# A fused delta-rule attention and two mixture-of-experts layers: the second layer's weight splits issued after the routing search's steps, and its last slot finished tile by tile

## The chip, the cores and the metric

One core of a Trainium2 chip. The metric is the device time of one execution in microseconds; three runs of the kernel before gave 959.33, 962.1 and 964.19, median 962.1.

## The reference, cut to what matters

Three stages follow one another: a delta-rule attention over 3072 tokens, a first expert layer, and a second expert layer, which is the one that the change touches. In it every token goes to one of 8 experts, each of which takes exactly 384 tokens; token and expert pairs are taken in falling order of their logits.

```python
cap = N // E                      # 3072 // 8 = 384
logits = x @ w_gate
for idx in np.argsort(-logits.flatten()):
    tok, e = int(idx) // E, int(idx) % E
    if assigned[tok] >= 0 or counts[e] >= cap:
        continue
    assigned[tok] = e
    counts[e] += 1
for e in range(E):
    mask = assigned == e
    h = np.maximum(x[mask] @ w1[e], 0.0)      # 384 -> 1024
    out[mask] = h @ w2[e]                     # 1024 -> 384
```

## The kernel before, in words

The second layer (`layer2`) runs eight *slots*, one per expert, in the order in which experts fill up. A *router* finds them: a *phase* of it searches the logit threshold at which the next expert is full (`search`), closes that expert (`close`) and lists its tokens (`listing`). A search has four *steps*. In each, DVE makes an index (`sf`, line 1382) and two comparison tables (`cmp`, 1333), PE counts with 24 small matmuls (`pr` <- `cmp`, 1341), DVE thresholds the counts (`reach`, 1345), PE spreads the result with one matmul (1351), and DVE reduces it (`reached`, 1355); then comes the next step's `sf`. After the fourth step `close` starts with `sel` (1474) and ends in `new` (1481), which a PE matmul waits for (1489). `listing` makes `clv` on DVE, from it POOL makes the expert's number `ei` (1541), SyncE (SP) reads that and issues four loads of 768 KB (`raw`, 1031 and 1034); later DVE makes `mrk` and `he`, PE lists (1570) and DVE writes the token indices `lidx` (1578).

A slot (`ffn`) is 48 *points*. A point is three matmuls of 384 columns, either part of the first product (`g1`, `ph` <- `xT`, line 1077; three points make one of eight blocks f) or of the second (`g2`, `po` <- `HL,hh`, line 1097; per block f and token tile t). A product is three matmuls because weights and activations are held as a high and a low part. After a block's third `g1` point ACT writes the high part of the activation `hh` (1080) and DVE the low part (1085, `h_low`). There are two `ph` buffers, so block f+2 cannot start before DVE has done block f's low part. `g2` of block f comes two blocks later (`LAG`); the last two blocks come at the end, tile by tile.

At every point `tasks(pt)` may put one piece of other work into the engines' queues: the router's next piece (`next(r)`; the numbers that the router yields, table `WT`, say how many points to let pass: the second is the wait from `cmp` to the count, the third from the count to `reach`), the loads (`load_ahead`), the gather of the next slot's tokens (`xg`) and its three transposes (`trans`, `xT`), and the *splits*. Each engine works its queue in order.

A split (`split_w`, lines 1047 and 1048) turns half a loaded piece of 128 x 1536 into its high part (ACT copies, `HL` <- `raw`) and its low part (subtraction `raw` - high, on DVE or on POOL). Eight splits j = 0 to 7 make the weights of one slot; they are done during the slot before, into the other of two `HL` buffers. In the kernel before, a slot's splits start 10 points after its four loads were put in the queue (2 points into the slot if that was at point 0 or earlier), are spread evenly to point 46, and the low part goes to POOL for j other than 1 and 5, to DVE for these two. In slot 0's own weights the two engines alternate. At a slot's end `finish2` copies the three output tiles `x` <- `po` (1594, 1596) and POOL issues three scatters (`out_dram`, 1599).

Of the kernel before, what the change touches and what calls it, by code (L numbers as in the profile page):

```python
# [35 lines left out]
class Attention:  # L36
# [369 lines left out]
    def go(self, w_gate, side=iter(())):  # L406
# [160 lines left out]
J = 64  # L567
STEPS = 4
LAG = 2
WT = [(5, 4, 1, 2, 3, 3, 1), (5, 4, 1, 2, 3, 3, 1), (5, 4, 1, 2, 3, 3, 1), (5, 4, 1, 2, 3, 2, 2),  # L570
      (5, 4, 1, 2, 3, 2, 2), (5, 4, 1, 2, 3, 3, 2), (5, 4, 1, 2, 6, 3, 2), (5, 4, 1, 2, 7, 4, 2)]
PRO = 16
SPQ, TRQ = (3, 10), (11, 12, 12)
XW = 19
# [1 line left out]
HEAT = (2, 5, 6, 7, 9)  # L576
HEAT1 = (3, 1, 1, 1, 0)
BEFORE = 10


def run(g):
# [92 lines left out]
class Moe:  # L674
# [421 lines left out]
        for n, (a, b) in enumerate(((0, 0), (0, 1), (1, 0))):  # L1096
            nc.tensor.matmul(self.po[s][t], h[:, a, r], W[:, 2 + i, b, c], start=(f == 0 and n == 0), stop=(f == 7 and n == 2))  # L1097

    def ffn(self, s, tasks):

        pt = 0
        for f in range(8):
            for k in range(3):
                self.g1(s, f, k)
                tasks(pt)
                pt += 1
            self.h_low()
            for t in range(3):
                if f >= LAG:
                    self.g2(s, f - LAG, t)  # L1110
                    tasks(pt)
                    pt += 1
        for t in range(3):
            for f in range(8 - LAG, 8):
                self.g2(s, f, t)
                tasks(pt)
                pt += 1
# [50 lines left out]
    def layer1(self):  # L1168
# [65 lines left out]
        self.logits_add(7)  # L1234
        self.warm(BEFORE)
        with self.tc.For_i(1, n, 1) as j:
# [121 lines left out]
    def search(self):  # L1358


        nc = self.nc
        y = self.small([128, 24], "sy", bufs=2)
        f = self.f = self.small([128, 24], "sf", I16)
        cmp = [None, None]

        def front():
            nc.vector.scalar_tensor_tensor(f, self.key, self.sc, self.low, op0=OP.mult, op1=OP.add)
            self.warm(self.heat[2])
            yield
            cmp[0] = self.compare(f, 0)  # L1370
            yield
            cmp[1] = self.compare(f, 1)
            yield
            nc.vector.scalar_tensor_tensor(y, self.key, self.sc, self.low, op0=OP.mult, op1=OP.add)
            yield

        yield from self.keys(front())
        yield self.W[0]
        for i in range(STEPS):
            pb = self.pb = yield from self.count(cmp, i + 1 == STEPS)  # L1380
            if i + 1 < STEPS:
                nc.vector.tensor_scalar(f, y, pb, float(J), op0=OP.subtract, op1=OP.mult)  # L1382
                cmp = [self.compare(f, h) for h in range(2)]
                if i + 2 < STEPS:
                    y2 = self.small([128, 24], "sy", bufs=2)
                    nc.vector.tensor_scalar(y2, y, pb, float(J), op0=OP.subtract, op1=OP.mult)
                    y = y2
                yield self.W[1]

    def find(self, f, digits):  # L1390
# [214 lines left out]
    def layer2(self):  # L1605
        nc = self.nc
        self.oscat, self.wanted, self.split_at, self.W, self.out_of, self.heat = [], [], 0, WT[0], -1.0e30, HEAT
        self.raw, self.xg, self.xT, self.idx, self.oids = {}, {}, {}, {}, {}

        def split(s, j):  # L1610
            self.split_w(s, j, j % 2 if s == 0 else j % 4 != 1)
            if j % 2:
                self.split_at += 1

        self.L2s = self.c1.tile([128, 24, 8], F32, name="L2s")
        r = self.router()
        next(r)
        nc.gpsimd.tensor_copy(self.L2s, self.L2)
        while 0 not in self.idx:
            next(r)  # L1620
            self.load_ahead()
        self.gather(0, self.x2buf, self.idx[0])
        sp, tr = iter(range(8)), iter(range(3))
        for q in range(PRO):
            next(r)
            self.load_ahead()
            for _ in range(SPQ.count(q)):
                split(0, next(sp))
            for _ in range(TRQ.count(q)):
                t = next(tr)  # L1630
                self.trans(0, t, f"po{t}")
        first = len(SPQ)
        self.heat = (0,) * 5
        for s in range(8):
            at, k, wt, j = None, 0, None, 0

            def tasks(pt):
                nonlocal at, k, wt, j, first
                if s == 0 and first < 8 and pt % 2 == 0:
                    split(0, first)  # L1640
                    first += 1
                next(r, None)
                self.load_ahead()
                if s == 0 and pt == 30:
                    self.oids[0] = self.oid(0)
                if s == 7:
                    return
                if wt is None and len(self.raw.get(s + 1, ())) == 4:
                    wt = 2 if pt == 0 else pt + 10
                elif wt is not None and j < 8 and pt >= wt and not (s == 0 and first < 8):  # L1650
                    split(s + 1, j)
                    j += 1
                    wt = pt + max(2, (46 - pt) // (9 - j))
                if at is None and s + 1 in self.idx:
                    self.gather(s + 1, self.x2buf, self.idx[s + 1])
                    at = max(pt + 10, 24)
                elif at is not None and k < 3 and pt >= at + 5 * k:
                    self.trans(s + 1, k)
                    k += 1

            self.ffn(s, tasks)
            if s < 7:
                while s + 1 not in self.idx:
                    next(r)
                if at is None:
                    self.gather(s + 1, self.x2buf, self.idx[s + 1])
                while j < 8:
                    self.load_ahead()
                    split(s + 1, j)
                    j += 1  # L1670
                while k < 3:
                    self.trans(s + 1, k, "pr" if k == 1 else "pt")
                    k += 1
                self.oids[s + 1] = self.oid(s + 1)
            self.finish2(s)
        self.general()
# [16 lines left out]
    def router(self):  # L1693

        def phase(p):
            if p < 7:
                yield from self.search()
            else:
                yield from self.keys()
                yield  # L1700
            yield from self.close(p)
            yield self.W[6]

        def steps(g):
            for n in g:
                for _ in range(n or 1):
                    yield

        side = iter(())
        for p in range(8):  # L1710
            self.W = WT[p]
            for _ in steps(phase(p)):
                next(side, None)
                yield
            for _ in side:
                yield
            side = steps(self.listing(p))
            if p in (0, 7):
                yield from side
                side = iter(())  # L1720
# [87 lines left out]
```

## Time and profile before

| what | value |
|---|---|
| median of three runs | 962.1 us |
| the profiled execution | 958.21 us, its span 956.3 us |
| second layer's slots | from about 668 us; slot 1 starts at 707.4, slot 5 at 870.6, slot 7 at 923.0, last product at 948 us |
| PE busy, whole span | 833.6 us (87%) |
| POOL low parts in the second layer | 46 splits, 1854 ns each |
| DVE low parts in the second layer | 18 splits, 1312 ns each |

PE, DVE, ACT and POOL are TensorE, VectorE, ScalarE and GpSimd; SPq is SyncE's queue. In a timeline row the first number is the start, the second the length, and the bracket the idle time of the engine before it with the work that ended it. PEclk is the TensorE clock that was granted, as a share of the full 2.4 GHz.

### The profile page before, as it was taken

Reading aid. Unit: us, or ns where it says so; the run is one execution under the profiler, and the core shown is the slowest. Engines: PE = TensorE matmul, PEld = TensorE weight load, DVE = VectorE, ACT = ScalarE, POOL = GpSimd, SP = SyncE. Lnnn points to the kernel's source line nnn. Section 1 sums busy time; section 2 is a strip of 40 time slices with the busy share of each in tenths; the row PEclk is TensorE's granted clock in tenths of the full one; section 3 lists DMA queues with packets and bytes.
Section 4 is the critical chain, followed back from the end, with each engine's and each line's share of the span. In section 5 each row is a group of like instructions: output and inputs, shape, how many; then the busy total and the mean of one; then the engine's idle time right before and its main releaser. Section 6 shows DMA issues by size and latency. Waiting matters only on the chain. (4 is left out here: it accounts for less than half of the span.)

```text
span 956.3 us, 23017 instructions
## 1 busy us (share of the span) xinstructions
PE 833.6 (87%) x9031; PEld 747.0 (78%) x9031; DVE 657.9 (69%) x1716; ACT 454.6 (48%) x990; POOL 381.7 (40%) x532
## 2 busy tenths in 40 slices
PE   5459879888897996999999999987989879989996
PEld 4448769777786885799999999864768768879996
DVE  5997989899797958555745556238767886785331
ACT  4556576675766576344445454221243232333431
POOL 7256345453432022522122221023474556457551
PEclk9878798897888798999999999999999999999998
DMA  9651143351500004563185532203245225326300
GB/s 156 117 99 35 39 90 68 69 106 39 102 19 19 20 28 160 202 207 115 33 296 162 151 115 77 90 29 111 69 145 175 92 92 183 132 66 234 117 25 28
DMA packets 141318, 98.27 MB, mean 103 GB/s; under 512 B 102757, under 2 KB 123268, under 8 KB 141204
## 3 DMA queue, kind: packets, MB, share of 16 engines
q1 hardware_dynamic: 134484, 76.67, 29.7%
q0 software_dynamic: 6720, 20.07, 6.6%
q8 instruction: 74, 1.21, 0.5%
q14 instruction: 40, 0.33, 0.1%
HBM read 82.36 MB, written 14.55 MB: 101 GB/s over the span
## 5 line engine op out<-in xcount | busy, mean ns | idle before, releaser
L1097 PE MATMUL po<-HL,hh 128*128 128x384 f32 x1152 | 235.9, 345 | 0.0
L1077 PE MATMUL ph<-xT,HL 128*128 128x384 f32 x1152 | 231.9, 344 | 3.0 <-ACT xT L1066 1.2
L1077 PEld LDWEIGHTS ph<-xT,HL 128*128 128x128 f32 x1152 | 200.3, 189 | 15.1 <-issue 6.7
L1097 PEld LDWEIGHTS po<-HL,hh 128*128 128x128 f32 x1152 | 199.2, 190 | 3.2 <-issue 1.3
L1080 ACT ACTIVATE hh<-ph 128x384 fp32r<-128x384 f32 x128 | 62.7, 491 | 174.6 <-PE ph L1077 153.5
L1085 DVE SCALAR_TENSOR_TENSOR hh<-ph,hh 128x384 fp32r<-128x384 f32 x128 | 70.7, 553 | 92.1 <-ACT hh L1080 76.3
L1048 POOL TENSOR_TENSOR HL<-raw,HL 128x768 fp32r<-128x768 f32 x52 | 95.2, 1850 | 58.1 <-ACT HL L1047 58.0
L1047 ACT ACTIVATE HL<-raw 128x768 fp32r<-128x768 f32 x128 | 105.2, 839 | 27.4 <-DMA raw<-in_moe_w_dram 27.2
L1048 DVE TENSOR_TENSOR HL<-raw,HL 128x768 fp32r<-128x768 f32 x76 | 79.0, 1040 | 48.0 <-ACT HL L1047 47.8
L280 DVE TENSOR_TENSOR Dtmp<-Dt 128x30 f32<-128x30 f32 (+22 forms) x199 | 89.8, 459 | 4.0
L284 DVE TENSOR_TENSOR Dt<-Dt,Dtmp 128x30 f32<-128x30 f32 (+22 forms) x199 | 81.0, 414 | 3.0
L379 PE MATMUL pc<-SI,R 112*48 112x56 f32 (+1 forms) x1536 | 64.6, 238 | 18.8 <-DVE R L357 14.5
L379 PEld LDWEIGHTS pc<-SI,R 112*48 112x48 f32 (+1 forms) x1536 | 56.7, 146 | 26.9 <-DVE R L357 17.8
L357 DVE TENSOR_TENSOR R<-pz,C 112x448 f32<-112x448 f32 x96 | 57.2, 615 | 20.0 <-ACT lgr L387 10.8
L1133 POOL DMA_INDIRECT x2buf<-x,pidx x24 | 23.8, 992 | 106.1 <-ACT x L1129 86.0
L353 PE MATMUL pz<-AT,Z 64*112 64x112 f32 x768 | 55.0, 288 | 7.3 <-ACT Z L343 7.2
L339 PE MATMUL pz<-RK,XT 128*128 128x96 f32 x384 | 60.1, 322 | 0.0
L232 PE MATMUL pa<-KQ 64*64 64x128 f32 x640 | 47.8, 297 | 11.7 <-ACT KQ L221 11.6
L339 PEld LDWEIGHTS pz<-RK,XT 128*128 128x128 f32 x384 | 55.9, 232 | 1.7
L353 PEld LDWEIGHTS pz<-AT,Z 64*112 64x112 f32 x768 | 46.1, 191 | 12.4 <-ACT Z L343 8.9
L232 PEld LDWEIGHTS pa<-KQ 64*64 64x64 f32 x640 | 39.0, 147 | 15.4 <-ACT KQ L221 12.5
L398 POOL COPY xt<-LG 128x8 f32<-128x8 f32 x24 | 4.9, 206 | 112.2 <-DVE LG L395 57.9
(408 smaller groups left out, 1300.7 us busy)
## 6 DMA issues: line engine op xcount, KB each, us to landing
raw<-in_moe_w_dram SPq DMA_DIRECT2D x68, 768.0 KB
xbuf<-xt SPq DMA_DIRECT2D x24, 196.0 KB
qt<-in_q_dram SPq DMA_DIRECT2D x22, 192.0 KB
kt<-in_k_dram SPq DMA_DIRECT2D x21, 192.0 KB
RK<-in_k_dram SPq DMA_DIRECT2D x48, 72.0 KB
RK<-in_v_dram SPq DMA_DIRECT2D x48, 72.0 KB
RK<-in_k_dram SPq DMA_DIRECT2D x8, 96.0 KB
RK<-in_v_dram SPq DMA_DIRECT2D x8, 96.0 KB
```

Of the source, the lines that this page charges most:

```text
L232: nc.tensor.matmul(pg[r, p], KQ[:, 0:64], KQ, start=True, stop=True)
L280: nc.vector.tensor_mul(t[:, i:k], X[:, j + 1 + i:j + 1 + k, j:j + 1].to_broadcast([128, k - i, j]), X[:, j:j + 1, :j].to_broadcast([128, k ...
L284: nc.vector.tensor_add(X[:, j + 1 + i:j + 1 + k, :j], X[:, j + 1 + i:j + 1 + k, :j], t[:, i:k])
L339: nc.tensor.matmul(pz[:, p], self.XT[0][:, u], self.RK[:, n % RSLOTS, u], start=True, stop=True)
L353: nc.tensor.matmul(self.pr[h][:, p], self.Z[r, u], self.AT[r, n % SLOTS, u, 64:176], start=True, stop=True)
L379: nc.tensor.matmul(self.pc[r, hd], self.Rb[n % 2][0:112, hd % 2, c, hd // 2, r], SI[0:112, hd], start=True, stop=True)
L1047: nc.scalar.activation(t[:, i, 0, c], self.raw[s][i][:, c], AF.Copy)
L1048: (nc.gpsimd if pool else nc.vector).tensor_sub(t[:, i, 1, c], self.raw[s][i][:, c], t[:, i, 0, c].bitcast(F32))
L1077: nc.tensor.matmul(self.ph, W[:, i, a, c], x[:, k, b], start=(k == 0 and n == 0), stop=(k == 2 and n == 2))
L1080: nc.scalar.activation(h[:, 0], self.ph, AF.Relu)
L1085: self.nc.vector.scalar_tensor_tensor(h[:, 1], ph, 0.0, h[:, 0].bitcast(F32), op0=OP.max, op1=OP.subtract)
L1097: nc.tensor.matmul(self.po[s][t], h[:, a, r], W[:, 2 + i, b, c], start=(f == 0 and n == 0), stop=(f == 7 and n == 2))
```

## The change

The splits of a slot are now held in a list `todo`. While the router searches, a split is issued only when the search has just put an `sf` and its two `cmp` into DVE's queue: `CALM` names, for the three places of a search, on which engine the low parts go and how many, one per point ("VP": one on DVE, then one on POOL; then twice "VVP"). While no search runs (phase 7 and after it) one split is issued every three points, on DVE. Splits 6 and 7 of a slot may run over into the slot itself. A slot's splits still become due 10 points after its loads were put in the queue, or at point 2 if that happens at point 0. The table `WT` lets one point more pass between `cmp` and count in phases 3 to 6, and one more between count and `reach` in phases 4 to 6. In slot 7 the last three blocks instead of the last two are left for the end of `ffn`.

```diff
-WT = [(5, 4, 1, 2, 3, 3, 1), (5, 4, 1, 2, 3, 3, 1), (5, 4, 1, 2, 3, 3, 1), (5, 4, 1, 2, 3, 2, 2),
-      (5, 4, 1, 2, 3, 2, 2), (5, 4, 1, 2, 3, 3, 2), (5, 4, 1, 2, 6, 3, 2), (5, 4, 1, 2, 7, 4, 2)]
+WT = [(5, 4, 1, 2, 3, 3, 1), (5, 4, 1, 2, 3, 3, 1), (5, 4, 1, 2, 3, 3, 1), (5, 5, 1, 2, 3, 2, 2),
+      (5, 5, 2, 2, 3, 2, 2), (5, 5, 2, 2, 3, 3, 2), (5, 5, 2, 2, 6, 3, 2), (5, 5, 2, 2, 7, 4, 2)]
...
+CALM = ("VP", "VVP", "VVP")
+KEPT = 6
...
-    def ffn(self, s, tasks):
+    def ffn(self, s, tasks, last=False):
...
+        end = 8 - LAG - last
...
-                if f >= LAG:
+                if f >= LAG and f - LAG < end:
...
-            for f in range(8 - LAG, 8):
+            for f in range(end, 8):
...
             pb = self.pb = yield from self.count(cmp, i + 1 == STEPS)
+            self.calm = ""
             if i + 1 < STEPS:
...
+                self.calm = CALM[i]
                 yield self.W[1]
...
+        def next_split(pool):
+            s2, j, _ = todo.pop(0)
+            self.split_w(s2, j, pool)
+            if j % 2:
+                self.split_at += 1
...
-                next(r, None)
+                searching = next(r, self) is not self and self.phase < 7
                 self.load_ahead()
+                if s < 7 and wt is None and len(self.raw.get(s + 1, ())) == 4:
+                    wt = 2 if pt == 0 else pt + 10
+                    todo.extend((s + 1, j, wt) for j in range(8))
+                if todo:
+                    s2, j, t = todo[0]
+                    if s2 == s:
+                        t, late = 0, pt >= 24
+                    else:
+                        late = j < KEPT and pt >= 40 + j
+                    if pt >= t and (self.calm or late or not searching and pt >= last + 3):
+                        next_split(self.calm[:1] == "P")
+                        self.calm = self.calm[1:]
+                        last = pt
...
-                if wt is None and len(self.raw.get(s + 1, ())) == 4:
-                    wt = 2 if pt == 0 else pt + 10
-                elif wt is not None and j < 8 and pt >= wt and not (s == 0 and first < 8):
-                    split(s + 1, j)
-                    j += 1
-                    wt = pt + max(2, (46 - pt) // (9 - j))
...
-            self.ffn(s, tasks)
+            self.ffn(s, tasks, s == 7)
...
-                while j < 8:
-                    self.load_ahead()
-                    split(s + 1, j)
-                    j += 1
+                while todo and todo[0][1] < KEPT:
+                    next_split(False)
+                last = 0
```

In the queues this comes to 19 low parts on POOL (46 before) and 45 on DVE (18 before): three on POOL and five on DVE for each of slots 1 to 5, all eight on DVE for slots 6 and 7, slot 0's as before. SyncE's queue has the same rows in the same order. Lines after 567 have numbers 2 to 28 higher in the changed kernel.

The first place is **DVE in slot 1, between two steps of a search**. `HL` rows are low parts of splits, `hh` rows the low parts of activations. Before:

```order
1258 L1382 TENSOR_SCALAR sf<-sy,bound 128x24
1259 L1333 TENSOR_TENSOR cmp_9454<-sf,tab_4718 128x768
1260 L1333 TENSOR_TENSOR cmp_9456<-sf,tab_4718 128x768
1261 L1386 TENSOR_SCALAR sy<-sy,bound 128x24
1262 L1085 SCALAR_TENSOR_TENSOR hh<-ph,hh 128x384
1263 L1067 TENSOR_TENSOR xT<-pt,xT 128x3x128
1264 L1345 TENSOR_SCALAR reach<-pr,rem_6225 8x64
1265 L1048 TENSOR_TENSOR HL_5216<-raw,HL_5216 128x768
1266 L1355 TENSOR_SCALAR reached,bound<-pr 128x64
1267 L1382 TENSOR_SCALAR sf<-sy,bound 128x24
```

Now:

```order
1260 L1387 TENSOR_SCALAR sf<-sy,bound 128x24
1261 L1337 TENSOR_TENSOR cmp_9455<-sf,tab_4718 128x768
1262 L1337 TENSOR_TENSOR cmp_9457<-sf,tab_4718 128x768
1263 L1391 TENSOR_SCALAR sy<-sy,bound 128x24
1264 L1050 TENSOR_TENSOR HL_5216<-raw,HL_5216 128x768 x2
1265 L1087 SCALAR_TENSOR_TENSOR hh<-ph,hh 128x384
1266 L1069 TENSOR_TENSOR xT<-pt,xT 128x3x128
1267 L1349 TENSOR_SCALAR reach<-pr,rem_6225 8x64
1268 L1087 SCALAR_TENSOR_TENSOR hh<-ph,hh 128x384
1269 L1069 TENSOR_TENSOR xT<-pt,xT 128x3x128
1270 L1359 TENSOR_SCALAR reached,bound<-pr 128x64
1271 L1387 TENSOR_SCALAR sf<-sy,bound 128x24
```

The one low part that stood right ahead of `reached` is gone from there; two now stand behind the comparison tables and ahead of `reach`.

The second place is **POOL at the start of slot 5**. `ei` is the number of an expert whose weights are still to be loaded. Before, where this `ei` is the one of slot 7 and slot 6's stands earlier, in slot 4:

```order
337 L1529 TENSOR_TENSOR clt<-cl,i_4552 128x8
338 L1530 TENSOR_SCALAR clt<-dr 128x8
339 L1531 COPY clt<-cl 128x8
340 L1541 TENSOR_SCALAR ei<-clv 128x1
341 L1545 TENSOR_SCALAR clv<-clv 128x1
342 L1546 TENSOR_TENSOR clv<-clv 128x1
343 L1547 TENSOR_TENSOR clv<-clv 128x1
344 L1548 TENSOR_TENSOR skip<-skip,clv 128x1
345 L1584 TENSOR_SCALAR oif<-skip 128x1
346 L1585 TENSOR_SCALAR oid<-xg,oif 128x3
347 L1598 MEMSET spacer 1x1
348 L1599 DMA out_dram<-x_11342,oid 3072x384
```

Now, where it is the one of slot 6:

```order
327 L1535 TENSOR_TENSOR clt<-cl,i_4552 128x8
328 L1536 TENSOR_SCALAR clt<-dr 128x8
329 L1537 COPY clt<-cl 128x8
330 L1590 TENSOR_SCALAR oif<-skip 128x1
331 L1591 TENSOR_SCALAR oid<-xg,oif 128x3
332 L1604 MEMSET spacer 1x1
333 L1605 DMA out_dram<-x_11200,oid 3072x384
334 L1604 MEMSET spacer 1x1
335 L1605 DMA out_dram<-x_11200,oid 3072x384
336 L1604 MEMSET spacer 1x1
337 L1605 DMA out_dram<-x_11200,oid 3072x384
338 L1547 TENSOR_SCALAR ei<-clv 128x1
```

The router has fallen back by half a slot, so that slot 6's expert number now stands at point 0 of slot 5, behind the three scatters of slot 4.

In the same stretch **ACT's queue** has, right behind slot 5's first `hh`, the high part of slot 6's first split (before, this split stood there too, with its loads issued at point 24 of slot 4):

```order
648 L1602 ACTIVATE x_11200<-po_10809 128x384
649 L1602 ACTIVATE x_11200<-po_10811 128x384
650 L1082 ACTIVATE hh<-ph 128x384
651 L1049 ACTIVATE HL_5216<-raw 128x768
652 L1082 ACTIVATE hh<-ph 128x384
653 L1049 ACTIVATE HL_5216<-raw 128x768
654 L1082 ACTIVATE hh<-ph 128x384
```

The split is put in at point 3, block 1's `hh` at point 5 stands behind it.

## Rows read from the trace of the kernel before

**Rows 1.** Busy time by stretch (length, engines, PEclk): slots 1–4, slot 5.
```profile
707.40:870.60 163.20, 141.18 (x1200) 125.43 (x1201) 127.61 (x381) 50.65 (x92) 91.93 (x123) 0.98 0.37 127
870.60:897.60 27.00, 27.00 (x179) 26.46 (x179) 10.65 (x24) 12.20 (x21) 18.50 (x18) 1.00 0.50 161
```

**Rows 2.** PE waits in slots 1–4 (total us, times, longest).
```profile
PE pr L1341 <- DVE cmp L1333: 9.2, 4, 3.1
PE pr L1489 <- DVE new L1481: 4.1, 4, 2.0
PE pr L1570 <- DVE he L1566: 1.2, 2, 0.6
PE pr L1351 <- DVE hh L1085: 1.9, 1, 1.9
PE pr L1351 <- DVE reach L1345: 1.4, 2, 1.2
```

**Rows 3.** Timeline (start, length): PE, POOL, DVE near the start of slot 1.
```profile
713.79 0.98 PE L1341 MATMUL pr<-cmp,ohu 128*8 128x64 bf16 x24 [3.06 <-DVE cmp L1333]
704.17 8.92 POOL L1048 TENSOR_TENSOR HL<-raw,HL 128x768 fp32r<-128x768 f32 x5
708.76 4.38 DVE L1382 TENSOR_SCALAR sf<-sy,bound 128x24 int16<-128x24 f32 x1
670.18 0.24 DVE L1382 TENSOR_SCALAR sf<-sy,bound 128x24 int16<-128x24 f32 x1
```

**Rows 4.** Groups by line, slots 1–4 (busy, mean ns | idle before).
```profile
L1474 DVE TENSOR_SCALAR sel<-jh,bound 8x64 f32<-8x64 f32 x5 | 4.1, 814 | 0.2
L1048 POOL TENSOR_TENSOR HL<-raw,HL 128x768 fp32r<-128x768 f32 x28 | 51.0, 1837 | 36.5 <-ACT HL L1047 36.4
L1047 ACT ACTIVATE HL<-raw 128x768 fp32r<-128x768 f32 x32 | 26.5, 837 | 12.3 <-DMA raw<-in_moe_w_dram 12.2
L1085 DVE SCALAR_TENSOR_TENSOR hh<-ph,hh 128x384 fp32r<-128x384 f32 x32 | 17.7, 552 | 11.3 <-ACT hh L1080 11.3
```

**Rows 5.** Timeline, DVE: one split beside an idle POOL.
```profile
781.50 0.96 DVE L1048 TENSOR_TENSOR HL<-raw,HL 128x768 fp32r<-128x768 f32 x1
```

**Rows 6.** Busy time by stretch, three pieces of 5 us.
```profile
715.00:720.00 5.00, 5.00 (x20) 4.22 (x19) 2.65 (x12) 1.07 (x3) 2.95 (x5) 0.66 0.32 120
775.00:780.00 5.00, 5.00 (x40) 4.61 (x38) 3.51 (x7) 2.21 (x4) 1.84 (x1) 1.00 0.02 5
785.00:790.00 5.00, 3.03 (x11) 3.02 (x11) 4.73 (x17) 1.22 (x2) 2.60 (x5) 0.71 0.00 0
```

**Rows 7.** Timeline: expert number, load and first split in slots 3 and 2.
```profile
793.71 0.46 POOL L1541 TENSOR_SCALAR ei<-clv 128x1 int32<-128x1 f32 x1 [2.56 <-DVE clv L1540]
794.98 0.37 SPq L1031 DMA_DIRECT2D raw<-in_moe_w_dram  x1
801.48 0.84 ACT L1047 ACTIVATE HL<-raw 128x768 fp32r<-128x768 f32 x1 [3.96 <-DMA raw<-in_moe_w_dram]
759.05 0.37 SPq L1031 DMA_DIRECT2D raw<-in_moe_w_dram  x1
763.72 0.85 ACT L1047 ACTIVATE HL<-raw 128x768 fp32r<-128x768 f32 x1 [4.34 <-DMA raw<-in_moe_w_dram]
```

**Rows 8.** Timeline around the start of slot 7, PE and POOL.
```profile
918.31 4.84 PE L1097 MATMUL po<-HL,hh 128*128 128x384 f32 x27
922.99 4.84 PE L1077 MATMUL ph<-xT,HL 128*128 128x384 f32 x27
925.56 0.98 POOL L1599 DMA_INDIRECT out_dram<-x,oid  x1 [0.26 <-ACT hh L1080]
```

**Rows 9.** Timeline, the end of slot 7, POOL and ACT.
```profile
946.84 0.98 POOL L1599 DMA_INDIRECT out_dram<-x,oid  x1 [20.21 <-ACT x L1596]
948.15 0.49 ACT L1596 ACTIVATE x<-po 128x384 f32<-128x384 f32 x1 [1.59 <-PE po L1097]
949.41 0.99 POOL L1599 DMA_INDIRECT out_dram<-x,oid  x1 [0.23 <-POOL spacer L1598]
```

More of the change, by code (lines that the diff above doesn't have):

```diff
@@ L1633, in layer2 @@
         self.heat = (0,) * 5
+        self.calm = ""
+        todo, last = [], 0
+        def next_split(pool):
[3 more added lines that the diff above has]
+                self.split_at += 1
         for s in range(8):
-            at, k, wt, j = None, 0, None, 0
+            at, k, wt = None, 0, None
             def tasks(pt):
-                nonlocal at, k, wt, j, first
+                nonlocal at, k, wt, last, first
                 if s == 0 and first < 8 and pt % 2 == 0:
-                    split(0, first)
+                    self.split_w(0, first, first % 2 > 0)
+                    if first % 2:
+                        self.split_at += 1
                     first += 1
-                next(r, None)
+                searching = next(r, self) is not self and self.phase < 7
                 self.load_ahead()
+                if s < 7 and wt is None and len(self.raw.get(s + 1, ())) == 4:
[11 more added lines that the diff above has]
+                        last = pt
                 if s == 0 and pt == 30:
@@ L1666, in layer2 @@
                     self.gather(s + 1, self.x2buf, self.idx[s + 1])
-                while j < 8:
-                    self.load_ahead()
-                    split(s + 1, j)
-                    j += 1
+                if wt is None:
+                    while len(self.raw.get(s + 1, ())) < 4:
+                        self.load_ahead()
+                    todo.extend((s + 1, j, 0) for j in range(8))
+                while todo and todo[0][1] < KEPT:
+                    next_split(False)
+                last = 0
                 while k < 3:
@@ L1710, in router @@
         for p in range(8):
-            self.W = WT[p]
+            self.W, self.phase = WT[p], p
             for _ in steps(phase(p)):
```

## The prediction

> **What bounds the kernel now.** I read three views in this order: busy time by stretch, to find where PE has room; PE's waits in that stretch, to see what fills it; then the timeline, to see why. In slots 1 to 4 of the second layer PE is busy 141.2 of 163.2 us, so 22.0 us are idle; in slot 5, where the search is over, it is busy 27.0 of 27.0 [rows 1]. So a gain has to come from slots 1 to 4, and whatever delays PE in slots 5 to 7 costs in full. Of the 22 us, 9.2 in four waits are PE waiting for the comparison tables, 4.1 for `new`, 1.2 for `he`, 3.3 for `hh` or `reach` [rows 2].
>
> Why DVE is late there is seen around 710 us. PE waits 3.06 us for `cmp`. The `sf` ahead of it took 4.38 us, where the same row elsewhere takes 0.24. POOL ran five splits without a break from 704.17 to 713.09, and `sf` ended 0.05 us after them [rows 3]. A DVE operation on SBUF that meets running POOL splits is held until they are through. `sel`, 0.24 us when alone by the same measure, took 4.1 us in five [rows 4].
>
> **The change, part by part.**
>
> *Collisions.* POOL keeps three splits a slot in slots 1 to 5, each put in two points or one after a step's `cmp`, so that it has the rest of the step. A step of phases 4 to 6 is 10 points long. A point lasts 0.52 us: slot 7's first product starts 4.68 us after the 27 matmuls before it [rows 8]. The split comes at the third point at the latest, its ACT copy takes 0.84, with two other copies ahead of it 2.5, and POOL 1.84 [rows 4]: it is done some 5 us after the step's `cmp`, before the next `sf`, which comes more than 5.2 us after. I count as removed the four `cmp` waits (9.2), the two `he` waits (1.2), and of `new` what `sel` was stretched, 4.1 - 5 x 0.24 = 2.9: together 13.3 us. Bounds: all of it, or two thirds (8.9) if one split in three still reaches into the next `sf`. I take 13.3, since the room is there.
>
> Here a rule can be set against the row. The Trainium skill (SBUF — State Buffer, Who interferes with whom) says that VectorE and GpSimd share a port pair that one of them holds for a whole instruction while the other is fully blocked. By that `sf` would have waited only for the third of the five splits, to about 709.5; the trace shows it held through the fifth. Priced by the rule, the 3.06 us wait would not count as a collision, the term would be 10.2, and my time 957.5.
>
> *Clock.* Behind the 3.06 us wait the granted clock was 0.66 for 5 us, behind a 2 us wait at 785 it was 0.71; behind another long wait at 771 it stayed 1.00 [rows 6]. In 5 us at 0.66 PE loses 1.7 us, at 0.71 1.45. These 3.1 us go with the waits. Ends: 0 and 3.1.
>
> *Splits moved to DVE.* 27 more low parts run on DVE, 0.96 us each when POOL is idle [rows 5]. Twelve are in slots 5 and 6, where DVE is busy 10.7 of 27 us [rows 1]: hidden; without that cover 11.5 us. Fifteen are done during slots 0 to 4, and in slots 1 to 4 DVE had 35.6 us free [rows 1] and gets back the collisions (4.1 on one `sf`, 2.9 on `sel`). 14.4 us fit. But they stand ahead of `reach`: two low parts (1.9) and one or two `hh` (0.55 each [rows 4]) behind the tables are about 3 us, and `reach` is not due before the fifth or sixth point plus the count (0.98 [rows 3]), 3.6 to 4.6 us after the step began. I cost that at nothing, except at the start of slot 1, where `sf`, tables, output copy, two splits and the first `hh` meet: 0.9 us. The upper end is the third rival's.
>
> *First split of a slot.* Its low part was on POOL and is now on DVE, and DVE's queue stands until the weights are there. From the load's issue to ACT's copy it took 4.7 and 6.5 us in two slots, and from `ei` to the issue 1.3 [rows 7]. In slots 2 to 4 the split is put in 11 points behind `ei`, and `ei` comes behind three scatters in slots 3 and 4. Adding 1.3, 4.7 to 6.5, copy 0.84, low part 0.96, `hh` 0.55, I get `reach` late by 0.1, 0.4 and 1.6 us in slots 2, 3 and 4. That is 2.1 in place of the 3.3 us of `hh` and `reach` waits [rows 2], so a gain of 1.2.
>
> *Slot 5.* This is the costliest step. The longer waits in `WT` add 3 points in phase 3 and 7 in each of phases 4 to 6, 24 in all. The router still ends inside slot 5 (last `lidx` at point 37), so that costs nothing in itself. But slot 6's `ei` falls on point 0 of slot 5, and there the rule "due at point 2" holds, which is meant for weights loaded long before. `ei` stands behind three scatters. At slot 7's start the third scatter ended 3.55 us after the slot's first product [rows 8]. So `ei` starts at about 3.8, the loads at 5.1, and ACT's copy begins at 9.8 to 11.6. That copy stands in ACT's queue ahead of block 1's `hh`, and its low part in DVE's ahead of block 1's low part: done at copy + 0.84 + 0.96 + 0.55, 12.1 to 13.9 us. PE needs it for block 3, at point 12, 6.2 us into the slot. PE waits 5.9 to 7.7 us; I take 6.8. Three of these splits then delay `he` of the listing by about 1.0, and the clock, which fell behind two of three long waits, costs 1.7. Together 9.5. Ends: 5.9 without the clock and the listing, 11.
>
> *End of slot 7.* The last tile is ready at the same time as before, the first one 6 matmuls earlier (1.04 us at 0.173). Before, the third scatter began at 949.41, behind the second, though its copy was done at 948.64 [rows 9]. The first scatter can begin 1.0 us earlier, the third then waits for its copy: 948.9, a gain of 0.5.
>
> **Sum.** -13.3 - 3.1 + 0.9 - 1.2 + 9.5 - 0.5 = -7.7 us. The profiled execution took 958.2, 3.9 less than the median 962.1 of the runs; from that I predict 962.1 - 7.7 = 954.4. A measurement of this kernel can tell about 0.5%, 4.8 us, from no change.
>
> **Rivals.**
>
> 1. *The weights come in time in slot 5* because POOL's scatters and `ei` run sooner than I think, or ACT's copy is not in the way. Then 9.5 falls away: 944.9. For it: PE never waited in slot 5 before [rows 1]. Against: there the loads had been issued half a slot earlier.
>
> 2. *Slot 5's wait is met in slots 2 to 4 too.* If loads land late (6.5 us and more, as in one of two [rows 7]) and queue behind the scatters, each of these three slots loses a further 2 us or so on DVE, since the first split no longer can wait on POOL. 954.4 + 6 = 960.4, no change that can be told. For it: ACT waited 12.2 us for `raw` in slots 1 to 4 [rows 4]. Against: PE showed only 3.3 us of it.
>
> 3. *DVE becomes the bound, slower.* If ACT's copy is not ahead of DVE, DVE idles for each copy (0.84) beside each low part (0.96) inside the search step, and there are 15 such steps. Less about 0.5 us of room that is 1.3 us a step, 19.5 in all: 974. It turns the sign as soon as a step loses 0.5 us (15 x 0.5 = 7.7). The Trainium skill (Perfetto Trace Analysis, Optimizing Scalar/DVE Operations) advises the way opposite to this change, to move work off a saturated DVE, even to GpSimd. For it: DVE is busy 127.6 of 163.2 us [rows 1]. Against: a good part of that is held time, and ACT is busy only 50.7.
>
> 4. *The collisions stay*, because POOL's splits drift into the next `sf`: half the 16.4 us are kept, 962.6, no change.
>
> **How the numbers follow.** My forecast has 0.52, its own range 949 to 959 by the bounds above. Rival 1 has 0.16, rival 2 0.12, rival 3 0.12, rival 4 0.08. A range of 943 to 964 holds rivals 1, 2 and 4 and leaves out rival 3 and little else. Faster by over 0.5% (under 957.3): rival 1 and most of my own, 0.63. Within 0.5%: the rest of my own, rivals 2 and 4, 0.25. Slower (over 966.9): rival 3, 0.12.
>
> **What would show it right or wrong.** In the changed profile: `sf`, `sel` and `cmp` near 0.24 and 0.55 us with no row over 2; PE's waits for `cmp` and `new` in slots 1 to 4 down from 13.3 to under 3 us; clock 1.00 there; POOL with 19 splits in the second layer. In slot 5 one wait of PE of 6 to 8 us for `hh`, with ACT idle until `raw` lands. The last scatter 0.5 us nearer the last product. It is wrong if PE's waits for `reach` grow by 0.5 us a step, or if slot 5 stays at 27 us.

## The result, and the profile after

The changed kernel takes 951.63 us (median of 4 runs, 951.34 to 951.87) beside 961.98 of the kernel before (4 runs, 959.33 to 964.19): ratio 0.989, 95% interval 0.987 to 0.992. It is faster by 10.3 us between the medians, and by 6.3 between the two profiled executions (951.86 and 958.21): the profiled execution of before was at the low end of its runs, that of the changed kernel at its median. In line numbers of the changed kernel, `sf` is 1387, `cmp` 1337, `reach` 1349, `sel` 1480, `new` 1487, the split 1049 (ACT) and 1050, `hh` 1082 and 1087. One count ahead of the prediction was off by one: the trace has 18 low parts on POOL in the second layer and 46 on DVE, where 19 and 45 were said (slot 1's weights have two on POOL, not three).

Busy time by stretch, slots 1 to 4 and slot 5 (beside [rows 1]; columns: stretch, length, busy time and count of PE, weight loads, DVE, ACT, POOL, then granted clock, DMA share, GB/s):

```profile
708.50:854.50 146.00, 138.27 (x1151) 122.11 (x1152) 111.39 (x357) 51.69 (x93) 63.96 (x90) 0.99 0.36 120
854.50:891.90 37.40, 31.07 (x229) 29.05 (x228) 22.19 (x68) 12.01 (x22) 12.22 (x28) 0.95 0.59 201
```

Slots 1 to 4 are 17.2 us shorter than before, slot 5 is 10.4 longer: three fifths of the gain are given back in one slot. PE's waits in slots 1 to 4 (beside [rows 2]; total, times, longest):

```profile
PE ph L1079 <- DVE hh L1087: 2.5, 1, 2.5
PE pr L1345 <- DVE ohu L1332: 1.9, 3, 0.9
PE pr L1495 <- DVE new L1487: 0.3, 1, 0.3
```

No wait for `cmp` is left (9.2 before), 0.3 for `new` (4.1). The groups of the same stretch show why (beside [rows 3, 4]; busy, mean ns, then idle before; the first line is `sf` of the kernel before, the others are of the changed kernel):

```profile
L1382 DVE TENSOR_SCALAR sf<-sy,bound 128x24 int16<-128x24 f32 x13 | 12.3, 944 | 0.5
L1387 DVE TENSOR_SCALAR sf<-sy,bound 128x24 int16<-128x24 f32 x13 | 3.1, 239 | 0.5
L1480 DVE TENSOR_SCALAR sel<-jh,bound 8x64 f32<-8x64 f32 x5 | 1.2, 243 | 0.2
L1050 DVE TENSOR_TENSOR HL<-raw,HL 128x768 fp32r<-128x768 f32 x22 | 26.4, 1227 | 3.4 <-ACT HL L1049 3.4
L1050 POOL TENSOR_TENSOR HL<-raw,HL 128x768 fp32r<-128x768 f32 x12 | 23.9, 1992 | 51.3 <-ACT HL L1049 51.3
```

In this stretch `sf` and `sel` now take their 0.24 us; on average `sf` took 0.94 and `sel` 0.81 before. Slot 5, timeline of POOL, SP, ACT, DVE and PE in this order (in brackets the idle time before the row, and what ended it):

```profile
857.79 1.05 POOL L1605 DMA_INDIRECT out_dram<-x,oid  x1 [0.25 <-issue]
858.92 0.23 POOL L1547 TENSOR_SCALAR ei<-clv 128x1 int32<-128x1 f32 x1
859.99 0.37 SPq L1033 DMA_DIRECT2D raw<-in_moe_w_dram  x1
864.94 0.84 ACT L1049 ACTIVATE HL<-raw 128x768 fp32r<-128x768 f32 x1 [8.68 <-DMA raw<-in_moe_w_dram]
865.82 0.96 DVE L1050 TENSOR_TENSOR HL<-raw,HL 128x768 fp32r<-128x768 f32 x1 [7.36 <-ACT HL L1049]
858.51 1.33 PE L1079 MATMUL ph<-xT,HL 128*128 128x384 f32 x6 [1.28 <-DVE hh L1087]
867.30 3.25 PE L1079 MATMUL ph<-xT,HL 128*128 128x384 f32 x9 [4.52 <-DVE hh L1087]
```

The chain is the one forecast: third scatter, `ei`, load, copy, low part, `hh`. PE stands for 4.5 us at its end, where 6 to 8 were forecast, and for another 1.3 us before. The nine matmuls behind it take 3.25 in place of some 1.7, at a granted clock of 0.71:

```profile
865.00:870.00 5.00, 2.70 (x8) 2.71 (x9) 4.18 (x10) 3.74 (x6) 0.00 (x0) 0.71 1.05 385
```

The end of slot 7, ACT and POOL (beside [rows 9]): the last scatter begins 0.76 us behind the last copy's start, 1.26 before.

```profile
942.62 0.49 ACT L1602 ACTIVATE x<-po 128x384 f32<-128x384 f32 x1 [2.66 <-PE po L1099]
943.38 0.98 POOL L1605 DMA_INDIRECT out_dram<-x,oid  x1 [0.40 <-ACTq L1455]
```

### The profile page after: what moved, and what is told of

Read it like the earlier page. It is cut to its first block, busy times and chain, and to the rows that moved or that the text cites. A ratio compares the mean times of both kernels' runs of the same rounds, so it can differ in the third digit from the quotient of the medians.

```text
span 950.1 us, 22994 instructions
## 1 busy us (share of the span) xinstructions
PE 834.7 (88%) x9024; PEld 746.8 (79%) x9031; DVE 657.3 (69%) x1744; ACT 454.1 (48%) x990; POOL 335.5 (35%) x504
## 5 line engine op out<-in xcount | busy, mean ns | idle before, releaser
L1099 PE MATMUL po<-HL,hh 128*128 128x384 f32 x1152 | 238.3, 345 | 0.2 <-DVE hh L1087 0.2
L1099 PEld LDWEIGHTS po<-HL,hh 128*128 128x128 f32 x1152 | 196.9, 189 | 3.6 <-issue 0.7
L1050 DVE TENSOR_TENSOR HL<-raw,HL 128x768 fp32r<-128x768 f32 x104 | 105.4, 1023 | 57.8 <-ACT HL L1049 57.4
L1050 POOL TENSOR_TENSOR HL<-raw,HL 128x768 fp32r<-128x768 f32 x24 | 46.4, 1942 | 64.3 <-ACT HL L1049 64.2
L353 PE MATMUL pz<-AT,Z 64*112 64x112 f32 x768 | 52.6, 279 | 7.4 <-ACT Z L343 7.3
L232 PE MATMUL pa<-KQ 64*64 64x128 f32 x640 | 49.0, 302 | 10.3 <-ACT KQ L221 10.2
L353 PEld LDWEIGHTS pz<-AT,Z 64*112 64x112 f32 x768 | 44.0, 184 | 12.5 <-ACT Z L343 9.2
L1605 POOL DMA_INDIRECT out_dram<-x,oid x24 | 25.6, 1066 | 55.9 <-ACT x L1602 46.1
```

The lines of the kernel that those rows point to most:

```text
L232: nc.tensor.matmul(pg[r, p], KQ[:, 0:64], KQ, start=True, stop=True)
L353: nc.tensor.matmul(self.pr[h][:, p], self.Z[r, u], self.AT[r, n % SLOTS, u, 64:176], start=True, stop=True)
L1050: (nc.gpsimd if pool else nc.vector).tensor_sub(t[:, i, 1, c], self.raw[s][i][:, c], t[:, i, 0, c].bitcast(F32))
```

## The experiments

The theory: POOL's splits hold DVE's operations, and taking most of them off POOL, at points where they end in time, makes the gain of slots 1 to 4; the late expert number makes the loss of slot 5. Rivals: the longer waits of `WT`, or the tie to the step, make the gain whatever the engine; and slot 5 is longer only because router work was moved into it. Each kernel's ratio, with its 95% interval, is to the kernel before, run on the same chip (its medians there: 959.1 to 961.1). The changed kernel's 951.63 us (0.987 to 0.992) were measured beside another set of runs of before (median 961.98), so where a run is set beside it, the intervals of the ratios decide.

**1. Splits for slot 6 later** (the changed kernel with)

```diff
+ had = len(self.raw.get(s + 1, ())) == 4
  searching = next(r, self) is not self and self.phase < 7
- wt = 2 if pt == 0 else pt + 10
+ wt = 2 if had else 18 if pt == 0 else pt + 10
```

> The changed kernel; only the eight splits for slot 6 come later: where the weights' loads were queued at point 0 itself, the first split is due at point 18 and not at point 2. My theory (PE waits in slot 5 for hh blocks that stand behind a copy of weights that have not landed): slot 5, 37.4 us in the changed kernel, loses the 4.5 us wait for hh and most of the slow clock behind it and falls to 31 to 32; the whole is 5 to 7 us faster, about 945.5. Rival (slot 5 is longer because the end of the router was moved into it): slot 5 stays at 36 or more, the whole within 1.5 us of the changed kernel. Second rival (the splits, 8 more points late, now press on slot 6): slot 5 falls but slot 6 grows from 26.1 by as much.

943.57 us (ratio 0.980, 0.974 to 0.987), 8.1 under the changed kernel, somewhat more than expected. In the traces 0.9 us of it is in slots 1 to 4, which the edit does not touch: there the clock fell in the changed kernel's execution and not in this one (more on it below). Slots 1 to 4, 5 and 6:

```profile
708.30:853.40 145.10, 136.42 (x1147) 120.10 (x1148) 110.88 (x354) 51.28 (x92) 63.82 (x88) 1.00 0.36 121
853.40:884.30 30.90, 29.37 (x230) 27.67 (x229) 22.95 (x71) 12.14 (x21) 14.92 (x29) 1.00 0.72 242
884.30:910.30 26.00, 26.00 (x155) 25.90 (x154) 13.86 (x20) 12.27 (x21) 7.42 (x12) 1.00 0.16 49
```

Slot 5 falls from 37.4 to 30.9 at full clock, slot 6 stays. The moved router work is there too: 230 matmuls in place of 179, which make PE's busy time 29.4 in place of 27.0. So of the 10.4 us, 6.5 go with the late splits (1.7 of them as clock), 2.4 are the rival's, and 1.5 are waits that stay (1.26 of them for `hh`, behind the closing of the seventh expert on DVE).

**2. Before, with all low parts of slots 1 to 7 on DVE** (points and waits as before)

```diff
- self.split_w(s, j, j % 2 if s == 0 else j % 4 != 1)
+ self.split_w(s, j, j % 2 > 0 and s == 0)
```

> The kernel before, its splits at their old points; only the low parts of slots 1 to 7 all run on DVE. Theory (POOL's splits hold DVE's operations, wherever they are put): sf and sel fall to about 0.24 us each, PE's waits for cmp in slots 1 to 4 go from 9.2 to under 3, and since slot 6's weights are called half a slot earlier than in the changed kernel, slot 5 stays near 27: 945 to 953. Rival A (the tie to the step is what makes the gain; low parts that stand ahead of sf or of the tables cost as much as collisions did): within 3 us of the kernel before. Rival B (DVE becomes the bound): slower, 965 or more, with PE's waits for reach grown.

948.51 us (0.987, 0.980 to 0.993). The engine alone gives this much, no less than the whole change. No PE wait for `cmp` is left in slots 1 to 4; what is left there is three waits for `hh`, of 5.6 us. Rivals A and B fall.

```profile
L1048 DVE TENSOR_TENSOR HL<-raw,HL 128x768 fp32r<-128x768 f32 x32 | 30.4, 953 | 12.1 <-ACT HL L1047 12.0
PE ph L1077 <- DVE hh L1085: 5.6, 3, 3.8
```

**3. The changed kernel, with before's engines** (same points)

```diff
- next_split(self.calm[:1] == "P")
+ next_split(j % 4 != 1)
...
- next_split(False)
+ next_split(todo[0][1] % 4 != 1)
```

> The changed kernel, splits at the same points, with the engine rule of before: six of a slot's eight low parts on POOL (37 more than half of all again). Theory (collisions): in the steps with three POOL splits these run some 5.5 us back to back from about 1 us behind the tables, in steps of 5.2 to 5.7 us, and hold the next sf: sf over 0.6 us on average, PE's cmp waits return, slots 1 to 4 go from 146 to 152 or more, the whole 955 to 963. Rival (the tie alone keeps splits out of the way, the engine does not matter): within 1.5 us of the changed kernel.

(POOL has 46 low parts, 28 more than in the changed kernel; the "37" is a slip.) 981.98 us (1.020, 1.014 to 1.026): 30 us slower than the changed kernel and 23 slower than before on the same chip, more than the theory's 955 to 963. The direction was right: slots 1 to 4 take 159.7 us, where 152 or more were expected. What the theory lacked was the clock (0.95 there) and slots 0, 5 and 6, where POOL's splits came back too (slot 1 starts 9.6 us later, slots 5 and 6 take 42.7 and 32.1). It was also wrong on the row: `sf` takes 0.32 us on average in slots 1 to 4, not over 0.6, and PE waits for `cmp` once, 3.6 us. Other rows meet the block. The three splits of a step, tied together, make one block on POOL, and a DVE row that meets it lasts as long. DVE and POOL, slots 2 and 4, and PE behind the second:

```profile
779.86 5.89 DVE L1391 TENSOR_SCALAR sy<-sy,bound 128x24 f32<-128x24 f32 x1
780.32 5.38 POOL L1050 TENSOR_TENSOR HL<-raw,HL 128x768 fp32r<-128x768 f32 x3
854.99 6.74 DVE L1337 TENSOR_TENSOR cmp<-sf,tab 128x768 bf16<-128x768 int16 x2
855.47 5.36 POOL L1050 TENSOR_TENSOR HL<-raw,HL 128x768 fp32r<-128x768 f32 x3
861.31 1.44 PE L1345 MATMUL pr<-cmp,ohu 128*8 128x64 bf16 x24 [3.58 <-DVE cmp L1337]
```

The first ends at 785.75 and the splits at 785.70; in the second pair PE's count, which needs the tables, starts 0.48 us behind the splits' end at 860.83. So the tie by itself is no cure.

**4. The changed kernel with before's `WT`**

```diff
- (5, 5, 1, 2, 3, 2, 2), (5, 5, 2, 2, 3, 2, 2), (5, 5, 2, 2, 3, 3, 2), (5, 5, 2, 2, 6, 3, 2), (5, 5, 2, 2, 7, 4, 2)
+ (5, 4, 1, 2, 3, 2, 2), (5, 4, 1, 2, 3, 2, 2), (5, 4, 1, 2, 3, 3, 2), (5, 4, 1, 2, 6, 3, 2), (5, 4, 1, 2, 7, 4, 2)
```

> The changed kernel with the old step lengths of phases 3 to 7 (7 or 8 points a step in place of 8 to 10). Theory: slot 6's expert is known in the middle of slot 4 again, so slot 5 loses its wait and falls from 37.4 to 27 to 28; but a step with three splits is 2 to 3 points shorter, and the tables and reach come late: slots 2 to 4 lose 3 to 9 of what they gained. Whole 945 to 951. Rival (the longer steps, not the splits, make the gain of slots 1 to 4): slots 1 to 4 back at 158 or more and the whole at 955 or above.

943.38 us (0.980, 0.974 to 0.986): undoing this part of the change gains another 8 us. Slots 1 to 4 keep their gain (146.4), slot 5 is 27.4 again:

```profile
709.00:855.40 146.40, 137.08 (x1197) 121.20 (x1198) 117.43 (x395) 50.97 (x92) 62.75 (x102) 1.00 0.42 141
855.40:882.80 27.40, 27.08 (x180) 26.48 (x179) 15.57 (x30) 12.26 (x21) 8.82 (x15) 1.00 0.48 159
```

The shorter steps cost PE 3.6 us in three waits for `reach`, much as expected, but at full clock.

**5. Before, with the new `WT` alone**

> The kernel before, with only the change's longer step waits (the table WT); splits and their engines as before. With the kernel before, the changed kernel and the changed kernel with the old waits this makes the square of splits by waits. Theory: POOL still has 35 splits in slots 1 to 5, so the collisions stay for the most part (cmp and new waits of PE at 7 us or more in slots 1 to 4), the longer steps give back at most 4 us there; and slot 6's expert is known only at slot 5's start, where the first split's copy (ACT) stands ahead of the hh blocks whichever engine makes the low part: slot 5 goes from 27 to 33 to 37. Whole 960 to 970, not faster than before. Rival (longer steps leave room for POOL's splits and make a good part of the gain): slots 1 to 4 under 154 and the whole at 957 or less.

977.86 us (1.017, 1.011 to 1.024): worse than the theory said. Slots 1 to 4 do not fall, they grow from 163.2 to 168.6, and slot 5 is 40.6:

```profile
706.60:875.20 168.60, 143.61 (x1147) 126.73 (x1148) 127.47 (x345) 50.27 (x90) 89.43 (x110) 0.95 0.31 104
875.20:915.80 40.60, 33.44 (x229) 32.01 (x229) 20.48 (x61) 12.03 (x21) 21.27 (x31) 0.86 0.55 185
```

PE still waits 9.4 us for `cmp` (one wait of 3.6 behind three splits in a row on POOL). So the square is complete: splits and end alone -16 us (run 4), waits alone +17, both -10. The waits cost 8 us on top of the splits.

This run also says what the tie did in run 3, which has the same engines and waits (and the new end of slot 7): the two intervals overlap. In the two traces slots 1 to 4 are 8.9 us shorter with the tie (159.7 for 168.6), and more than that is lost elsewhere: slot 1 starts 11.5 us later, slots 5 and 6 are 2.1 and 6.1 us longer. That run 3 is slower than the kernel before is thus not shown to be the tie's doing; the longer waits alone give most of it.

**6. Before, with the new end of slot 7 alone**

> The kernel before, with only the order of the last slot's last 18 blocks of matmuls changed (one block more of the second product is kept for the end, so that tiles end one after the other). Theory: the first scatter begins about 1 us earlier against the last product, so the third no longer queues behind the second: it begins 0.7 to 0.8 us after the third tile's copy on ACT began, 1.26 in the kernel before, so 0.5 us off the end; every other part as before. Too little for the time to show: 958 to 964. Rival (the scatters' own time sets the end, or the last tile is ready later): the third scatter begins 1.2 us or more behind that copy.

960.91 us in its one run, no difference by time. The trace has the term: the last scatter begins 0.77 us behind the last copy's start (1.26 before).

```profile
951.62 0.49 ACT L1597 ACTIVATE x<-po 128x384 f32<-128x384 f32 x1 [2.64 <-PE po L1097]
952.39 0.98 POOL L1600 DMA_INDIRECT out_dram<-x,oid  x1 [0.40 <-ACTq L1450]
```

**7. The changed kernel with `clt` and `ei` on DVE**

```diff
- nc.gpsimd.tensor_mul(t[:, 1], cl, C.i8)
+ nc.vector.tensor_mul(t[:, 1], cl, C.i8)
...
- nc.gpsimd.tensor_scalar(ei, v[:, 1:2], 7.0, None, op0=OP.min)
+ nc.vector.tensor_scalar(ei, v[:, 1:2], 7.0, None, op0=OP.min)
```

> The changed kernel; four small operations of a listing (the three that fill clt, and ei) run on DVE instead of POOL, so that they no longer stand behind the three scatters of the slot before. Theory (my slot 5 term is a queue on POOL, then a load, then a copy): ei at slot 5's start comes 2.4 us sooner, so do the loads and ACT's copy, and PE's 4.5 us wait for hh falls to about 2; at slot 4's start DVE no longer waits 1.1 us for clt, and the 2.5 us wait there falls by 1 us or more. Whole 3 to 5 us faster than the changed kernel, 946.5 to 948.5. Rival (the transfer is late for another reason, or it is the closing chain on DVE that holds PE): within 1.5 us of the changed kernel, PE's wait in slot 5 at 4 us or more.

950.11 us (0.987, 0.982 to 0.991; runs 944.1 to 951.3): 1.5 us under the changed kernel, which the intervals can't tell apart, and by the time at the rival's edge. The trace tells more. The queue was as I said: slot 6's loads are issued at 857.64, 2.35 us sooner, the copy begins 1.8 sooner, and the wait of 4.5 is 1.0:

```profile
863.12 0.84 ACT L1049 ACTIVATE HL<-raw 128x768 fp32r<-128x768 f32 x1 [6.81 <-DMA raw<-in_moe_w_dram]
865.47 1.85 PE L1079 MATMUL ph<-xT,HL 128*128 128x384 f32 x9 [1.02 <-DVE hh L1087]
869.96 0.75 PE L1576 MATMUL pr<-he,o 128*32 128x12 f16 x24 [1.59 <-DVE he L1572]
```

But `he` is now 1.6 us late, and the clock fell twice, to 0.66 for 5 us each, so that PE is busy for 32.3 us, 2.9 more than run 1 at full clock, where the changed kernel lost 1.7:

```profile
860.00:865.00 5.00, 4.46 (x39) 3.77 (x37) 1.01 (x2) 1.89 (x4) 0.00 (x0) 0.66 0.96 337
870.00:875.00 5.00, 5.00 (x40) 4.97 (x40) 4.75 (x18) 0.40 (x2) 1.22 (x2) 0.66 0.02 3
```

Slot 5 is 36.5. Slot 4 falls from 37.2 to 34.8. Of these 2.4 us only 0.9 are the wait at its start, now 1.64 for 2.52; 1.5 are PE's busy time (33.1 for 34.6), that is, the clock, which stayed at 1.00 here.

```profile
824.08 1.84 PE L1079 MATMUL ph<-xT,HL 128*128 128x384 f32 x9 [1.64 <-DVE hh L1087]
```

The queue on POOL is shown, the expected time is not.

**8. The same on the old waits** (runs 4 and 7 together)

> The changed kernel with the old step waits, and with clt and ei on DVE. With the old waits an expert is known in the middle of a slot, away from the scatters in all slots but one, so by my theory little is left to gain: 0 to 2 us faster than with the old waits alone (943.4). Rival (the four operations on DVE stand ahead of the tables and cost more there than POOL's queue did): 1 us slower or more.

942.78 us (0.980, 0.977 to 0.983; runs 940.5 to 947.0): nothing that can be told from run 4.

**9. Half of the longer waits, and run 1's edit** (`WT` of phases 3 to 6 with 4 points behind the tables, as before; one more between count and `reach` in 4 to 6, as changed)

> The changed kernel with half of the longer waits: one point more between count and reach in phases 4 to 6, the wait behind the tables as before the change, and the splits for slot 6 due late where the loads are only just queued. Theory: the old waits cost 3.6 us of PE waiting for reach in slots 1 to 4, and one point (0.52 us) more in each of those steps removes about 2 us of that, while slot 6's expert is known at point 35 of slot 4, so that slot 5 stays near 27.5: 940.5 to 943. Rival (steps of 8 to 9 points only push router work into slot 5, where nothing is hidden): 944 or more, slot 5 at 29 or above.

939.16 us (0.977, 0.974 to 0.980), a little under the expected 940.5, and the fastest of all kernels here, 12.5 us under the changed one; it is 4 under runs 1 and 4, whose intervals overlap with its own.

```profile
707.80:850.90 143.10, 136.86 (x1173) 120.79 (x1174) 114.29 (x379) 50.99 (x92) 65.15 (x98) 1.00 0.39 129
850.90:879.10 28.20, 28.02 (x204) 27.14 (x203) 18.42 (x46) 12.26 (x21) 10.26 (x19) 1.00 0.69 235
```

No PE wait for `reach` is left in slots 1 to 4, and slot 5 is 28.2. Run 1's edit has no part in this. With these waits slot 6's loads are issued from 846.70 on, in slot 4, so the late rule does not apply, and the first copy begins 2.2 us into slot 5:

```profile
846.70 0.37 SPq L1033 DMA_DIRECT2D raw<-in_moe_w_dram  x1
853.06 0.83 ACT L1049 ACTIVATE HL<-raw 128x768 fp32r<-128x768 f32 x1
```

**10. Run 9 without POOL** (`CALM = ("VV", "VVV", "VVV")`)

> The kernel with half of the longer waits and the late splits of slot 6 (939.2 us), its 15 low parts on POOL in slots 1 to 5 now on DVE too. Theory (POOL is worth using as long as its splits end before the next sf; DVE has room for two low parts a step and not for three): a third low part of 0.96 us stands ahead of reach in some ten steps and delays it by 0.3 to 0.6 us: 942 to 946, PE's waits for reach at 3 us or more in slots 1 to 4. Rival (POOL's help is not needed, and what is left of the collisions goes): 936 to 940.

940.04 us (0.979, 0.976 to 0.982), where 942 to 946 were expected: no difference from run 9. PE waits once for `reach`, 1.1 us. My theory that DVE has no room for a third low part a step falls for steps of 8 to 9 points; that the three POOL splits of a slot are harmless stands.

**11. The first split on POOL** (the changed kernel with `CALM = ("PV", "VVP", "VVP")`)

> The changed kernel with the first two low parts of slots 2 to 5 exchanged: the first, which waits for its weights, on POOL, the second on DVE a point later. This measures the term that I called the first split of a slot. Theory: DVE's queue no longer stands until the weights are there (saves the 0 to 1.6 us that I gave a slot), but the second low part now runs beside POOL's first and takes about 1.96 in place of 0.96, so little comes of it: 950 to 953. Rival (DVE's wait for the weights is what holds PE at the start of the slots): 949 or less, PE's waits for hh down by 2 us or more outside slot 5. Second rival (the stretched split delays reach): 954 or more.

956.67 us (0.996, 0.992 to 0.999; 10 runs, 952.7 to 964.2), slower than the changed kernel, the second rival's case: slots 1 to 4 take 148.2. From 700 us on PE waits twice for `reach`, 3.2 us together (1.5 of it in slots 1 to 4). DVE's 46 low parts take 1.19 us on average, 1.11 in the changed kernel.

**12. Run 4 without POOL** (`CALM` as in run 10)

> The changed kernel with the old step waits (943.4 us) and with no low part of slots 1 to 7 on POOL. Beside the kernel before with all low parts on DVE at their old, even points (948.5) it differs in the points of the splits and in the last slot's end alone, so it tells what the tie to the step is worth by itself. Theory (the engine is the larger part, the tie keeps low parts from standing ahead of reach, new and he): 942 to 946. Rival (with POOL out of the way the points don't matter): 947 to 950. Second rival (three low parts a step on DVE are too many for steps of 7 and 8 points): 950 or more, PE's waits for reach in slots 1 to 4 over 5 us.

942.55 us (0.982, 0.978 to 0.987). Beside run 2 the tie is worth 6 us, but the intervals overlap (run 2: 0.980 to 0.993), so its size stays open. Beside run 4 the last POOL splits are worth nothing.

## Why the prediction was right, and where it was off

*Collisions: right.* The waits of which I counted 13.3 us away (`cmp`, `new` and `he`, 14.5 in all) are 0.3 in slots 1 to 4. Runs 2 and 3 show the cause from both sides: the new points take 951.6 us with most low parts on DVE and 982.0 with most on POOL, the old points take 948.5 with DVE. The bound "one split in three still reaches the next `sf`" was not needed, since each step had at most one on POOL.

The one place where the row spoke against a rule was decided by run 3. The Trainium skill (SBUF — State Buffer, Who interferes with whom) has one engine hold the shared port pair for a whole instruction while the other is blocked. I read that as a wait for one instruction; here `sy` and `cmp` were held through three POOL instructions, 5.4 us, as `sf` was before [rows 3]. Of its advice on a full DVE (Perfetto Trace Analysis, Optimizing Scalar/DVE Operations) the prediction gave half: the Trainium skill says that moving some work even to GpSimd may make sense, and adds that between these two it might not help. Run 3, which moves 28 low parts from DVE to POOL at the same points, cost 30 us.

*Clock: near by luck.* PE's busy time in slots 1 to 4 fell by 2.9, near the 3.1. But 0.7 of it is router work moved to slot 5 (run 4 beside run 1, both at full clock: 137.08 and 136.42). And the changed kernel still loses 1.85 us there (138.27 - 136.42), 1.45 of it in slot 4 (34.60 - 33.15), behind the 2.5 us wait at its start. I took the clock to go with the waits. It does not in every execution: run 1 has the same wait behind the same 18 matmuls, and its clock stayed at 1.00. Run 1's row, then 5 us of the changed kernel and of run 1:

```profile
823.52 1.86 PE L1079 MATMUL ph<-xT,HL 128*128 128x384 f32 x9 [2.51 <-DVE hh L1087]
820.00:825.00 5.00, 2.48 (x9) 2.43 (x9) 3.13 (x11) 0.49 (x1) 3.35 (x9) 0.77 0.29 89
820.00:825.00 5.00, 2.49 (x14) 2.17 (x13) 3.87 (x16) 0.52 (x2) 4.05 (x11) 1.00 0.20 79
```

So a difference between two executions of 1 to 2 us at one wait may be the clock alone.

*Start of slot 1 and first split: wrong terms, together small.* No wait of over 0.7 us is in slot 1, where I had 0.9. In slots 2 to 4 I had DVE waiting for weights, 0.1, 0.4 and 1.6 us; the wait that came, 2.5 us at slot 4, is another. DVE's `clv` stood 1.09 us for POOL's `clt`, which was behind three scatters, the second of which had waited for DVE's own output copy:

```profile
820.00 1.26 POOL L1605 DMA_INDIRECT out_dram<-x,oid  x1 [0.24 <-issue]
821.66 0.18 POOL L1537 COPY clt<-cl 128x8 f32<-128x8 f32 x1
821.88 0.18 DVE L1546 TENSOR_REDUCE clv<-clt 128x3 f32<-128x24 f32 x1 [1.09 <-POOL clt L1537]
822.57 3.17 PE L1079 MATMUL ph<-xT,HL 128*128 128x384 f32 x9 [2.52 <-DVE hh L1087]
```

Run 7 takes `clt` out of that queue, and the 2.5 us are 1.6; what makes the rest of that wait stays open. I had named the scatters as what is ahead of `ei`, and not asked who else waits for POOL there.

*Slot 5: right in its mechanism, +10.4 for +9.5, and in its size partly by luck.* By parts: waits for `hh` 5.8 (I said 6.8), for `he` and the gathered rows 0.6 (1.0), clock 31.07 - 29.37 = 1.7 (1.7), and 29.37 - 27.00 = 2.4 for some 50 matmuls of the router, which I had said cost nothing. My reason was that the router still ends inside the slot; but PE has no room there, and its work adds to the slot's length. Taking these matmuls out of slots 1 to 4 gained only 0.7 of busy time there; why not as much stays open.

The wait that I forecast, for the `hh` behind the late split, is 4.5, under my 5.9 to 7.7. The chain's times were about right: `ei` began 5.0 us into the slot (853.95), where I said 3.8, ACT's copy 11.0 (9.8 to 11.6), and PE went on at 13.35 (12.1 to 13.9). But PE came to block 3 at 8.8 us and not at 6.2, held up by the other 1.3 us wait for `hh` and by the router's matmuls. Two terms that I had at nothing, 1.3 and 2.4, made up for it.

*End: right*, 0.5, by the trace of run 6.

*Sum.* -17.2 + 10.4 - 0.5, and 1.1 us by which everything ahead of slot 1 was later in this execution, make the span's -6.2. The terms were to give -7.7, so 950.5 for the profiled execution, which took 951.9, 1.4 more. The forecast of 954.4 added the 3.9 us between before's profiled execution and its median; the changed kernel has no such gap. The two errors have opposite signs and make 2.5 of the miss of 2.8. The range of 949 to 959 was not what its bounds add up to: the low end of slot 5 alone gives 950.8, and the high ends of collisions, clock and slot 5 together 963.4.

*What I did not ask* is what the longer waits are for. I priced their side effect (9.5) and left their benefit inside the first term. Run 4 shows that this benefit is next to nothing (slots 1 to 4 146.4 for 146.0): the gain was all in the splits. Rival 3, DVE as the bound, is out: with every low part of slots 1 to 7 on DVE, runs 10 and 12 are faster than the changed kernel, and run 2 is not slower. Rival 1's time (944.9) is about what runs 1 and 4 reach.

## What to carry to other kernels

Where two engines hold each other up, look at the longest unbroken chain on the one and at what meets it on the other; its total of busy time says little. When a schedule is stretched, look for constants that were tuned to where things used to fall ("at point 0 the weights are there"), and for who waits behind the step that moved. A change of several parts should be run part by part: here one part cost 8 us, and with half of it the kernel was 12 us faster. And where the clock differs between two executions, compare waits and busy time apart before a gain is given to an edit.

## What the runs showed of the hardware

DVE rows were held for the whole of three POOL splits in a row (5.89 us on a row that takes 0.22 elsewhere in that trace), and came free when the last one ended, not the first. Not every DVE row is held: while the five splits of [rows 3] ran, the rows of the kernel before that read what PE had written took their usual times, and only `sf`, which reads SBUF alone, stood. So what the prediction says of "a DVE operation on SBUF" is shown for rows of that kind, and not for all that touch SBUF.

```profile
704.85 0.27 DVE L1345 TENSOR_SCALAR reach<-pr,rem 8x64 bf16<-8x64 f32 x1 [1.92 <-PE pr L1341]
707.57 0.55 DVE L1067 TENSOR_TENSOR xT<-pt,xT 128x384 fp32r<-128x384 f32 x1
```

And the clock behind a PE wait did not follow the wait's length: in slot 5, run 7 had waits of 1.6, 1.0 and 1.6 us and two stretches at 0.66, the changed kernel 1.3 and 4.5 us and one at 0.71; and a 2.5 us wait was followed by 0.77 in the changed kernel and by 1.00 in run 1. (Such a mean over 5 us lies between the two levels, 1.2 and 2.4 GHz, which are 0.5 and 1.) What decides it stays open.
